# Fourteen instead of eight half tiles of one token quarter's gate and up products inside the last seven segments, with a new table of priorities

## The chip, the cores and the metric

The kernel runs on one core of a Trainium2 chip. The metric is the device time of one execution in microseconds (us). Engines are named as the profile names them: PE (TensorE, matrix products; PEld is its loading of weights), DVE (VectorE), ACT (ScalarE), POOL (GpSimd), SP (SyncE, which mostly issues DMA transfers). SPq and ACTq are the issue of DMA transfers by SP and ACT.

## The reference

Everything is in bf16, with x of 2048 tokens by 640. A layer norm feeds part A, an attention that walks over 64 segments of 32 tokens with 8 memory rows; the memory rows of a segment's output are the memory of the next one, so the segments are strictly one after the other. Part B is a gated network on the layer norm of the sum.

```
for s in range(64):                                  # part A, on layernorm(x)
    h = concatenate([mem, x[32*s : 32*s+32]])        # 40 rows of 640
    q, k, v = h @ Wq, h @ Wk, h @ Wv                 # 32 heads of 128
    p = softmax(masked(q @ k.T * scale))             # the mask is causal among tokens
    o = (p @ v) @ Wo
    mem, out[s] = o[:8], o[8:]
h = x + out
n = layernorm(h)                                     # part B, F = 1728
result = h + (relu(n @ W_gate) * (n @ W_up)) @ W_down
```

## The kernel before, in words

One chain of segments sets the pace. In each segment PE multiplies 32 rows (8 memory rows and the segment's first 24 tokens) with Wq, Wk and Wv (line L1577, 32 columns of the array per matmul and four side by side), takes scores (L1954, L1958), the sums of the exponentials (L1968), the weighted values (L1993, L1998), the product with Wo for the rows that the next segment needs (L2027, L2046) and the sum that turns to the next memory (L2063, L1555). The remaining eight tokens of each segment are handled for several segments together: their q, k and v in `rest`, their output rows in `rest_o` (L1661, written to memory by `rest_out`, L1675). A block z is 128 tokens, four segments; z runs from 0 to 15.

Part B works on quarters of 512 tokens. F is cut into 14 tiles of 128 columns (the last of 64). `ahead` (L1726) computes one half tile, gate or up of one tile, inside a segment, while PE still has the segments' work to do: five chunks of four matmuls of 32 columns each (L1742), 20 in all. It loads that tile's weights by SP (L1731) into Wgs or Wus, one buffer each; the gate half is evacuated with a relu (L1750), the up half multiplied to it (L1756) and the tile stored to scr_g (L1758). The table GXS says for each of the first three quarters from which segment to which, and how many half tiles. Quarters 0 and 1 run 27 each (all of them) in segments 21 to 55; quarter 2 runs eight, declared in segments 56 to 62 (the second number is not included; the scheduler may place the work later). What is not computed early follows behind the last segment.

The end part consists of `gates` (L1761) for what is left of quarter 2 and all of quarter 3, and `downs` (L1809), the product with W_down, for each quarter. In `gates` a tile is two groups of five matmuls that use the whole array (L1778), evacuated by ACT (relu, L1800) and DVE (product, L1802). Its first tile is `done`, half the third entry of GXS (L1765); the tiles computed early are loaded back from scr_g into gT (L1767). Block 15's output rows are inserted ahead of the tile `done + 3` (L1785 to L1788). The order of the calls is gates(2), downs(2), downs(0), downs(1), gates(3), downs(3).

The weights of the end part share memory with Wq, Wk, Wv and Wo, so they can be loaded only as those come free. `load_f` (L2160) issues them on SP: Wg and Wu come in three pieces of columns, FPIECES; the first piece waits for Wq's last use, the others also for the evacuation of the last segment's output:

```
FPIECES = ((512, 896), (896, 1664), (0, 512))
for n, (f0, f1) in enumerate(FPIECES):
    for wt, src, nm in ((Wg, B_W_gate, "Wg"), (Wu, B_W_up, "Wu")):
        load_f(..., ["B0"] + [("osb", 1)] * (n > 0), D * (f1 - f0) * 2)
```

Tiles 4 to 6 are columns 512 to 895, tiles 7 to 12 are 896 to 1663, and tiles 0 to 3 are 0 to 511. W_down (Wd, L2169) follows them, then the narrow last tile (Wl) and the results of quarters 0 and 1 (gTs, L2177).

No order is written out by hand. Every operation is declared with `op(...)`, its name, its inputs and its buffers; a list scheduler (`_Sched`, L817) then goes through modelled time and picks, engine by engine, the ready operation of the highest level: the longest path to the end plus a bias from the table BIAS, by name ("gx") and by name and segment ("gx@57"), in L985 and L986. The table ENGINE says which of ACT and DVE an evacuation runs on. Each engine then runs its list strictly in order, with semaphore waits. Within one SP list a transfer that waits holds back every transfer behind it.

At the start the first tokens are loaded and normalised, and Wq, Wk and Wv arrive chunk by chunk; PE meanwhile runs the early blocks of `rest` beside segment 0. Their q and k are stored to scr_qk by DMAs that ACT issues (L1607), their v to scr_v by SP (L1624).

Of the kernel before, what the change touches and what calls it, by code (L numbers as in the profile page):

```python
# [20 lines left out]
GXS = ((21, 38, 27), (39, 55, 27), (56, 63, 8))  # L21
# [6 lines left out]
BIAS = {"sel2": -428.53, "ezero": 827.13, "ldxs0": 772.6, "ldxs1": -1075.19, "ldxa": 977.15, "ldxl": -444.97,  # L28
    "ldxx": 94.56, "ldxn": 296.11, "ldxx0": -425.81, "ldxst": -946.28, "ldxxm": -329.88, "ldmev": -440.02,
# [18 lines left out]
    "gx": -75.13, "gxrelu": -736.07, "gxev": -228.23, "gxst": -268.67, "ln2nd": -1166.07, "xnld": 1080.06,  # L48
    "gld": -294.56, "gu": 52.5, "relu": 1032.72, "gmul": -789.51, "roz": -16.73, "tn2go": 142.03,
# [1214 lines left out]
def build_kernel(nc, A_x, A_mem0, A_Wq, A_Wk, A_Wv, A_Wo, A_seg_len, B_x, B_W_gate, B_W_up,  # L1264
# [46 lines left out]
    sel2 = ar.alloc("sel2", [128, 64], BF16)  # L1311
# [21 lines left out]
    oTr = [ar.alloc(f"oTr{i}", [128, H, 32], BF16) for i in range(2)]  # L1333
# [547 lines left out]
    for nm, b in (("ldxr", 9000.0), ("ldxr1", 8950.0)):  # L1881
        for t in ("", "s0", "s1", "a", "l", "x", "n", "T", "e"):
            sc.bias[nm + t] = b
# [369 lines left out]
```

## Time and profile before

| | us |
|---|---|
| median of 3 runs | 998.62 |
| lowest, highest | 998.56, 999.2 |
| profiled execution | 995.62 |
| its span | 993.9 |
| PE busy in the span | 973.8 |
| end of segment 0 | 86.95 |
| end of segment 55 | 788.07 |
| end of segment 62 | 861.71 |
| end of segment 63 | 874.21 |

The end of a segment is the start of the first PE group behind its last L1555 matmuls, in the span's time. A row of the timeline gives the start, the length, engine, line, operation, the tiles (out<-in), the number of instructions, and in brackets the idle time ahead of it with what ended it. Lengths of neighbouring PE groups overlap, because matmuls are pipelined; what a group costs is the time from its start to the start of the next one. Rows of DMA issue (SPq, ACTq) give the time that the issuing engine spent; how long a transfer takes to land is in a separate view.

### The profile page before, as it was taken

To read this page: it belongs to the slowest core of one execution; us is meant where nothing else is said; L and a number is where in the kernel's file an instruction comes from. 1 tells how busy PE (TensorE), PEld (TensorE's weight loads), DVE (VectorE), ACT (ScalarE), POOL (GpSimd) and SP (SyncE) were. 2 spreads that over 40 slices of the span, in tenths; PEclk is the share of its full clock that TensorE was granted. 3 is DMA by queue.
4 is the path that set the end of the run, shared out by engine and by line. 5 is a ranking of instruction groups with operands and counts; after the bars stand their busy time and mean duration, and the time that the engine had idled before them with its cause. 6 is when DMAs were issued, how large, how long until landed. Compare 5 with 4: busy or idle time off the path is not lost.

```text
span 993.9 us, 54620 instructions
## 1 busy us (share of the span) xinstructions
PE 973.8 (98%) x25518; PEld 535.7 (54%) x24540; DVE 618.3 (62%) x1345; ACT 502.4 (51%) x1226; POOL 112.5 (11%) x264
## 2 busy tenths in 40 slices
PE   7989999999999999999999999999999999999998
PEld 4334565555555555655555556555555565543343
DVE  5835767768676766576666676767656766523232
ACT  2236555556565565555555565555555656521020
POOL 2341011111011011001000010000100000100000
PEclk9999999999999999999999999999999999999999
DMA  8996122223131323232232234333223352289211
GB/s 320 403 350 145 45 57 57 66 53 92 36 89 39 85 76 83 55 81 66 67 84 62 78 105 86 86 93 79 52 72 89 76 102 76 68 260 288 72 41 40
DMA packets 181553, 103.62 MB, mean 104 GB/s; under 512 B 126212, under 2 KB 177484, under 8 KB 181324
## 3 DMA queue, kind: packets, MB, share of 16 engines
q1 hardware_dynamic: 175948, 95.51, 34.5%
q10 hardware_dynamic: 5376, 4.63, 1.4%
q8 instruction: 196, 3.21, 1.3%
q14 instruction: 33, 0.27, 0.1%
HBM read 67.30 MB, written 29.75 MB: 98 GB/s over the span
## 4 chain that ended last, share of the span: by engine, by line
PE 90%; DMA 4%; SPq 3%; DVE 1%; issue 1%; ACT 0%; POOL 0%; ACTq 0%; DVEq 0%; POOLq 0%
PE ps L1577 49%; PE ps L2046 7%; PE ps L1742 7%; PE ps L2027 7%; PE ps L1834 4%; PE ps L1661 3%; PE ps L1778 3%; PE ps L1993 3%; DMA scr_qk<-stg 3%; PE ps L1555 2%; PE ps L1968 2%; PE ps L1954 1%; SPq L2164 1%; DMA Wq<-in_A_Wq_dram 1%; DMA scr_o<-osr 1%
## 5 line engine op out<-in xcount | busy, mean ns | idle before, releaser
L1411 ACT ACTIVATE tok<-ps 128x512 bf16<-128x512 f32 x216 | 128.2, 597 | 146.5 <-PE ps L1577 141.4
L1577 PE MATMUL ps<-Wk,xT 128*32 128x512 bf16 x2560 | 180.4, 379 | 0.4 <-ACT tok L1411 0.4
L1577 PE MATMUL ps<-Wv,xT 128*32 128x512 bf16 x2560 | 176.3, 379 | 0.0
L1577 PE MATMUL ps<-Wq,xT 128*32 128x512 bf16 x2560 | 170.1, 379 | 0.5 <-DVE tok L1412 0.3
L2076 DVE STREAM_TRANSPOSE QT<-tok 128x512 bf16<-128x512 bf16 x128 | 90.6, 708 | 47.5 <-ACT tok L1411 45.4
L1577 PEld LDWEIGHTS ps<-Wq,xT 128*32 128x32 bf16 x2560 | 70.6, 97 | 66.5 <-DVE xT L1691 9.1
L2076 DVE STREAM_TRANSPOSE KT<-tok 128x512 bf16<-128x512 bf16 x128 | 90.8, 709 | 24.6 <-ACT tok L1411 22.7
L1577 PEld LDWEIGHTS ps<-Wk,xT 128*32 128x32 bf16 x2560 | 68.4, 96 | 55.6 <-DVE xT L1691 2.9
L1963 ACT ACTIVATE E<-ps 128x224 bf16<-128x224 f32 x128 | 45.7, 357 | 81.4 <-PE ps L1958 77.7
L2046 PE MATMUL ps<-Wo,oT 128*32 128x160 bf16 x4096 | 83.5, 233 | 1.0 <-issue 1.0
L2046 PEld LDWEIGHTS ps<-Wo,oT 128*32 128x32 bf16 x4096 | 74.1, 97 | 15.5 <-ACT oT L1411 5.6
L2027 PE MATMUL ps<-Wo,oT 128*32 128x320 bf16 x2048 | 81.5, 300 | 0.9 <-DVE oT L1412 0.8
L1577 PEld LDWEIGHTS ps<-Wv,xT 128*32 128x32 bf16 x2560 | 61.0, 96 | 38.8 <-ACT tok L1411 0.7
L1412 DVE CAST oT<-ps 128x320 bf16<-128x320 f32 x124 | 55.0, 485 | 42.9 <-PE ps L1998 36.9
L1940 POOL COPY QT<-RS 128x256 bf16<-128x256 bf16 x64 | 25.7, 402 | 470.4 <-PE ps L1958 470.2
L1411 ACT ACTIVATE Vm<-ps 128x512 bf16<-128x512 f32 x122 | 72.0, 591 | 11.4 <-PE ps L1577 6.3
L1412 DVE CAST tok<-ps 128x512 bf16<-128x512 f32 x104 | 68.7, 661 | 9.6 <-PE ps L1577 9.3
L2027 PEld LDWEIGHTS ps<-Wo,oT 128*32 128x32 bf16 x2048 | 52.7, 96 | 27.3 <-DVE oT L1412 7.7
L1688 DVE CAST_PREDICATED xm<-turn,ps 128x64 bf16<-128x64 uint16 x126 | 27.9, 222 | 61.3 <-PE ps L1555 61.1
L2011 POOL COPY oTr<-oT 128x128 bf16<-128x128 bf16 x128 | 41.0, 320 | 193.5 <-ACT oT L1411 110.4
L1411 ACT ACTIVATE oT<-ps 128x320 bf16<-128x320 f32 x132 | 50.4, 436 | 11.5 <-PE ps L1998 11.1
L1411 ACT ACTIVATE ps<-seed 128x384 f32<-128x384 bf16 x117 | 54.4, 489 | 2.1 <-DVE half L2035 1.8
(108 smaller groups left out, 1453.5 us busy)
## 6 DMA issues: line engine op xcount, KB each, us to landing
RS<-scr_qk SPq DMA_DIRECT2D x63, 128.0 KB, 2.3
big<-in_A_x_dram SPq DMA_DIRECT2D x34, 160.0 KB, 2.8
Wq<-in_A_Wq_dram SPq DMA_DIRECT2D x10, 512.0 KB, 7.7
Wk<-in_A_Wk_dram SPq DMA_DIRECT2D x10, 512.0 KB, 8.2
Wv<-in_A_Wv_dram SPq DMA_DIRECT2D x10, 512.0 KB, 8.6
Wo<-in_A_Wo_dram SPq DMA_DIRECT2D x8, 640.0 KB, 11.2
Wgs<-in_B_W_gate_dram SPq DMA_DIRECT2D x30, 160.0 KB, 3.0
Wus<-in_B_W_up_dram SPq DMA_DIRECT2D x30, 160.0 KB, 2.9
```

What stands on the lines that cost most here:

```text
L1411: return e.activation(dst, src, ACTF.Copy)
L1412: return e.tensor_copy(dst, src)
L1577: o = pe.matmul(out, lhs[c], rhs, start=(c == 0), stop=(c == DC - 1), skip_group_check=True)
L1661: o = pe.matmul(bank(bk)[p0:p0 + 32, 0:2 * SLICE], oTr[b][:, h, :], cols(h, 2 * a, 2 * a + 2), start=(h < 2), stop=(h >= H - 2), skip_grou ...
L1742: o = pe.matmul(bank(bk)[32 * i:32 * i + 32, 0:512], wt[:, c, 32 * i:32 * i + 32], xn2T[0][:, :, c * 128:(c + 1) * 128], start=(c == 0), s ...
L1778: o = pe.matmul(bank(bk)[:, 0:TB], lhs(c), xT[:, :, c * 128:(c + 1) * 128], start=(c == 0), stop=(c == DC - 1))
L1834: pe.matmul(bank(ba)[:, 0:512], lhs, Wd[:, j, 0:512], start=(j == 0), stop=(j == FC - 1), skip_group_check=True)
L1963: op("act", lambda a: a.activation(E[:, g, :, 0:56], sco(BS[g]), ACTF.Exp, scale=SCALE), r=["table"], w=[("E", g)], x=[BS[g]], dur=0.36, n ...
L2011: op("pool", lambda e: e.tensor_copy(oTr[ob][:, 16 * g:16 * g + 16, XR * y:XR * y + XR], oT[:, 16 * g:16 * g + 16, 0:XR]), r=[("oT", g, 0) ...
L2027: o = pe.matmul(bank(BA)[p0:p0 + 32, 0:2 * SLICE], oT[:, h, XR:40], cols(h, 2 * b2, 2 * b2 + 2), start=(i == 0 and jj < 2), stop=(i == 3 a ...
L2046: o = pe.matmul(bank(BW)[32 * j:32 * j + 32, 0:SLICE], oT[:, 16 + 4 * jj + i, XR:40], cols(h, j, j + 1), start=(i == 0 and jj == 0), stop= ...
L2076: op("dve", lambda v, tb=tb, dst=dst: v.transpose(dst, tok[tb.at][:, :].rearrange("p (h r) -> p h r", r=32)), w=[("QT" if p == 0 else "KT" ...
```

## The change

The third entry of GXS becomes 14, so `done` becomes 7: tiles 0 to 6 of quarter 2 run inside the segments, two half tiles in each of seven, and gates(2) begins at tile 7. gT is loaded with seven tiles instead of four, and block 15's output rows stand ahead of tile 10 instead of tile 7. FPIECES is unchanged. Both tables, BIAS and ENGINE, are replaced in whole, some 750 lines of numbers, and the biases of the first loads (names that begin with ldxr) can now be set by the table.

```diff
-GXS = ((21, 38, 27), (39, 55, 27), (56, 63, 8))
+GXS = ((21, 38, 27), (39, 55, 27), (56, 63, 14))
...
-BIAS = {"sel2": -428.53, "ezero": 827.13, "ldxs0": 772.6, "ldxs1": -1075.19, "ldxa": 977.15, "ldxl": -444.97,
...
     for nm, b in (("ldxr", 9000.0), ("ldxr1", 8950.0)):
         for t in ("", "s0", "s1", "a", "l", "x", "n", "T", "e"):
-            sc.bias[nm + t] = b
+            sc.bias[nm + t] = BIAS.get(nm + t, b)
```

How the new tables move instructions shows only in the order that the scheduler makes of them. The counts of PE's instructions differ in two lines alone: 1360 for 1240 of L1742, 200 for 230 of L1778. Behind the last segment PE's list before is gates(2) from tile 4 (Wg x10, Wu x5, Wg x5, Wu x10, ...), block 15's output rows, the last tiles, 40 of block 14's output-row matmuls, downs(2). After, it is the last 8 gate and 20 up matmuls of tile 6 by `ahead`, then gates(2) from tile 7 (Wg x10, Wu x5, Wg x5, Wu x10), block 15's output rows, Wg x10, Wu x5, Wg x5, Wu x10, downs(2), with the narrow last tile inside downs(2); block 14's output rows all stand in the segments.

SP's list after, around the end of segment 63: first pieces of Wg and Wu, Wgs and Wus of tile 6, the store of tile 5, block 14's output rows, second pieces of Wg and Wu one behind the other (the first of them waits for the evacuation of the last output), two transposed loads (L1771), the store of tile 6, two loads for block 14's layer norm, the last segment's output, third pieces of Wg and Wu, gT, the store of block 14's sum, Wd, Wl. Before, one second piece stands ahead of the two transposed loads and the other behind them, and gT stands behind Wd and Wl.

At the start, ACT's list holds the exponentials of segment 0 (L1963) ahead of the last block of scr_qk stores instead of behind it, that block has five stores behind V's fourth evacuation instead of seven, and the two copies of the first normalised tokens (xr) are on DVE instead of one on ACT. On PE both sums of segment 0 (L1968) stand ahead of the V products of Wv with xr.

More of the change, by code (lines that the diff above doesn't have):

```diff
@@ L27 @@
 FPIECES = ((512, 896), (896, 1664), (0, 512))
-BIAS = {"sel2": -428.53, "ezero": 827.13, "ldxs0": 772.6, "ldxs1": -1075.19, "ldxa": 977.15, "ldxl": -444.97,
-    "ldxx": 94.56, "ldxn": 296.11, "ldxx0": -425.81, "ldxst": -946.28, "ldxxm": -329.88, "ldmev": -440.02,
[18 rows of a table removed]
-    "gx": -75.13, "gxrelu": -736.07, "gxev": -228.23, "gxst": -268.67, "ln2nd": -1166.07, "xnld": 1080.06,
-    "gld": -294.56, "gu": 52.5, "relu": 1032.72, "gmul": -789.51, "roz": -16.73, "tn2go": 142.03,
[632 rows of a table removed]
-ENGINE = {"ldxre": "act", "ldxr1e": "act", "ldmev": "act", "er0ev": "dve", "er0Tev": "act", "er1ev": "act",
-    "ervev": "act", "r0ev": "dve", "r0Tev": "act", "r1ev": "act", "rvev": "dve", "Q0ev": "act", "Q0Tev": "act",
-    "K0ev": "act", "K0Tev": "act", "V0ev": "act", "Q1ev": "dve", "Q1Tev": "dve", "K1ev": "act", "K1Tev": "act",
-    "seed0": "act", "seed1": "act", "oTev0": "dve", "oTev1": "act", "osrev": "act", "ldxre@0": "act",
[81 rows of a table removed]
+BIAS = {"sel2": -468.5, "ezero": 397.8, "ldxrs0": 9556.22, "ldxrs1": 9299.62, "ldxra": 8157.09,
+    "ldxrl": 8663.75, "ldxrx": 9076.13, "ldxrn": 9101.63, "ldxrT": 9580.86, "ldxre": 9514.39, "ldxs0": 2261.81,
+    "ldxs1": -1029.95, "ldxa": 854.49, "ldxl": -268.86, "ldxx": 357.13, "ldxn": 223.78, "ldxx0": -48.42,
[20 rows of a table added]
+    "gx": -76.02, "gxrelu": -589.09, "gxev": 150.7, "gxst": -333.11, "ln2nd": -1210.98, "xnld": 1157.81,
+    "gld": 118.19, "gu": -305.11, "relu": 1424.28, "gmul": -365.48, "roz": -5.91, "tn2go": 413.61,
[634 rows of a table added]
+ENGINE = {"ldxre": "dve", "ldmev": "act", "er0ev": "dve", "er0Tev": "act", "ervev": "act", "r0ev": "dve",
+    "r0Tev": "act", "r1ev": "act", "Q0Tev": "act", "K0Tev": "act", "Q1ev": "dve", "Q1Tev": "dve",
+    "K1Tev": "act", "seed0": "act", "seed1": "act", "oTev0": "dve", "oTev1": "act", "osrev": "act",
[84 rows of a table added]
 class _Slot:
```

1469 rows, old and new, of tables (BIAS, ENGINE) are left out of this document.

## The prediction

> **What bounds the kernel now.** I read the page's busy shares and chain first, then TensorE's timeline through the last segments and the tail, then the DMA queue's own timeline beside it, and last the start.
>
> ```profile
> span 993.9 us, 54620 instructions
> PE 973.8 (98%) x25518; PEld 535.7 (54%) x24540; DVE 618.3 (62%) x1345; ACT 502.4 (51%) x1226; POOL 112.5 (11%) x264
> PE 90%; DMA 4%; SPq 3%; DVE 1%; issue 1%; ACT 0%; POOL 0%; ACTq 0%; DVEq 0%; POOLq 0%
> ```
>
> TensorE is busy for 98% of the span and is 90% of the chain. What is left for a reordering is its idle time, so I asked for its busy time by stretches: start and segment 0; segments 1 to 55; 56 to 62; tail, with segment 63 left out. Columns are window, length, then PE, PEld, DVE, ACT and POOL.
>
> ```profile
> 0.00:86.95 86.95, 75.10 (x1521) 35.86 (x1513) 49.23 (x93) 31.96 (x72) 26.80 (x54) 0.98 0.98 332
> 86.95:788.07 701.12, 697.93 (x20684) 401.85 (x20004) 479.13 (x1067) 403.51 (x1000) 76.57 (x186) 1.00 0.29 72
> 788.07:861.71 73.64, 73.64 (x2197) 44.13 (x2118) 45.66 (x101) 44.40 (x109) 6.30 (x18) 1.00 0.35 79
> ...
> 874.21:993.90 119.69, 115.05 (x786) 47.38 (x572) 36.67 (x68) 16.48 (x31) 0.00 (x0) 1.00 0.47 143
> ```
>
> Segments 56 to 62, into which the change puts work, have no idle TensorE time (73.64 of 73.64 us). Idle time is found in the start (11.85 us), in 1 to 55 (3.19 us in 55 segments) and in the tail (4.64 us). Whatever is moved into the late segments lengthens them by its own cost.
>
> **The half tiles.** Six more half tiles run early: the order of TensorE's instructions holds 120 more of L1742 (32 columns of weights, four side by side) and 30 fewer of L1778 (128 columns); every other matmul count is as before. Their prices are start to start, from these rows:
>
> ```profile
> 849.44 1.03 PE L1742 MATMUL ps<-xn2T,Wgs 128*32 128x512 bf16 x16
> 850.30 0.60 PE L1577 MATMUL ps<-Wk,xT 128*32 128x512 bf16 x8
> ...
> 874.21 2.33 PE L1778 MATMUL ps<-xn2T,Wg 128*128 128x512 bf16 x10
> ...
> 878.54 2.32 PE L1778 MATMUL ps<-xn2T,Wu 128*128 128x512 bf16 x10
> 880.70 2.32 PE L1778 MATMUL ps<-xn2T,Wg 128*128 128x512 bf16 x10
> 884.22 1.25 PE L1778 MATMUL ps<-xn2T,Wu 128*128 128x512 bf16 x5 [1.21 <-DMA Wu<-in_B_W_up_dram]
> ```
>
> 16 of L1742 take 0.86 us, 0.054 each; 10 of L1778 take 2.16 us, 0.216 each. So 120 x 0.054 = 6.5 us are added and 30 x 0.216 = 6.5 us removed: 0 on TensorE. The six evacuations (three relu, three multiply) that change places go where ScalarE is busy 44.40 and VectorE 45.66 of 73.64 us; both cover them, and uncovered each would cost some 0.6 us. The six weight loads of 160 KB and three stores of 128 KB fall where the DMA share is 0.35; I count them 0, and return to them among the rivals.
>
> **What the order does at the end of segment 63.** Call that end T (874.21 before). The last early half tile is not finished at T: 28 of its matmuls stand behind it, 28 x 0.054 = 1.5 us. Then the first product of the third quarter's rest is tile 7, no longer tile 4. The weights come in three pieces of columns; the first, issued early, holds tiles 4 to 6, which this quarter no longer needs. Tile 7 is in the second piece, and that piece is issued only when the last segment's output has been evacuated. The rows of DMA issue and of the evacuation, and then the queue's medians from issue to landing:
>
> ```profile
> 874.32 0.30 ACT L1411 ACTIVATE osb<-ps 128x160 bf16<-128x160 f32 x1 [1.75 <-PE ps L1555]
> ```
> ```profile
> 874.65 0.37 SPq L2164 DMA_DIRECT2D Wg<-in_B_W_gate_dram  x1
> 875.06 2.94 SPq L1771 DMA_TRANSPOSE xn2T<-scr_n  x2
> 878.04 0.58 SPq L2164 DMA_DIRECT2D Wu<-in_B_W_up_dram  x1
> ...
> 879.38 0.59 SPq L2164 DMA_DIRECT2D Wg<-in_B_W_gate_dram  x1
> 880.02 0.76 SPq L2164 DMA_DIRECT2D Wu<-in_B_W_up_dram  x1
> 880.82 6.12 SPq L2164 DMA_DIRECT2D Wd<-in_B_W_down_dram  x2
> ```
> ```profile
> Wd<-in_B_W_down_dram SPq DMA_DIRECT2D x1, 2080.0 KB, 13.3
> Wg<-in_B_W_gate_dram SPq DMA_DIRECT2D x1, 960.0 KB, 5.3
> Wu<-in_B_W_up_dram SPq DMA_DIRECT2D x1, 960.0 KB, 6.1
> Wg<-in_B_W_gate_dram SPq DMA_DIRECT2D x1, 640.0 KB, 6.7
> Wu<-in_B_W_up_dram SPq DMA_DIRECT2D x1, 640.0 KB, 7.9
> ```
>
> Landings before, from T: gate piece two 874.65 + 5.3 = T + 5.7; up piece two T + 9.9; gate piece three T + 11.9; up piece three T + 13.7; Wd T + 19.9. Transfers of one queue land one after the other: 640 KB in 1.84 us (348 KB per us), and 3360 KB from T + 9.9 to T + 19.9 (337).
>
> Before, tile 4's products cover the first landing, and TensorE waits only for the up piece: 880.70 to 884.22 is 3.52 us for 2.16 us of matmuls, 1.4 lost. In the changed order:
> - Gate piece two still lands at T + 5.7; TensorE is done at T + 1.5. Wait: 4.2 us. Behind it in order stand the rest of the gate and up products and the second part's output rows, none of which can pass it.
> - Ten gate products, to T + 7.9. The up piece is now issued right behind the gate piece, not behind the transposes: 960 KB / 340 = 2.8 us later, T + 8.6. Wait: 0.7.
> - 50 products at 0.216 and 64 output-row matmuls, which took 2.3 us:
>
> ```profile
> 892.96 2.36 PE L1661 MATMUL ps<-Wo,oTr 128*32 128x320 bf16 x64
> 895.25 1.25 PE L1778 MATMUL ps<-xn2T,Wg 128*128 128x512 bf16 x5
> ...
> 910.17 0.39 PE L1834 MATMUL ps<-Wd,gT 128*128 128x512 bf16 x1 [0.36 <-DVE osr L1670]
> ```
>
>  That ends at T + 21.7, and the down products follow, which need Wd. On the queue Wd now stands behind gT (896 KB, not 512 and not after Wd), the last early tile's store (128 KB) and two rows' loads (320 KB): from T + 8.6, (3360 + 1344) / 337 = 14.0 us, T + 22.6, up to T + 23.5 if the transposes' 320 KB take their turn in it too. Wait: 0.9 to 1.8; I take 1.2.
>
> Sum of these waits: 4.2 + 0.7 + 1.2 = 6.1 us. Gone are the 1.4 above and the 0.36 at 910.17, since the output rows of that block come earlier. The tail therefore loses 6.1 - 1.8 = 4.3 us; the bounds are 4.2 - 1.8 = 2.4 (the other two waits vanish) and 5.0 (Wd at T + 23.5).
>
> **The start.** The new priorities also reorder the start, which the description hardly mentions. In the old one, TensorE and ScalarE:
>
> ```profile
> 58.65 9.88 PE L1577 MATMUL ps<-Wv,xr 128*32 128x512 bf16 x176
> 70.07 0.25 PE L1968 MATMUL ps<-E,bones 128*32 128x160 bf16 x4 [1.55 <-ACT E L1963]
> ...
> 70.75 2.12 PE L1577 MATMUL ps<-Wv,xr 128*32 128x512 bf16 x20 [0.39 <-ACT lnS L1976]
> 73.45 4.95 PE L1577 MATMUL ps<-Wv,xr 128*32 128x512 bf16 x80 [0.58 <-ACT stg L1411]
> 78.24 1.25 PE L1577 MATMUL ps<-Wq,xr 128*32 128x512 bf16 x20
> 80.29 1.05 PE L1577 MATMUL ps<-Wq,xr 128*32 128x512 bf16 x16 [0.80 <-DVE tok L1412]
> ```
> ```profile
> 66.00 3.61 ACTq L1607 DMA_DIRECT2D scr_qk<-stg  x5
> ...
> 72.81 0.60 ACT L1411 ACTIVATE stg<-ps 128x512 bf16<-128x512 f32 x1 [1.74 <-DMA scr_qk<-stg]
> ```
>
> The first exponential (L1963) stands in ScalarE's order behind the block of stores that it issues from 66.00 on (3.61 us for 5, 0.72 each), and the sums that need it stop TensorE: 58.65 + 176 x 0.054 = 68.15, next start 70.07, 1.9 lost; 0.5 more by 70.75. Then V's products wait for their evacuations, which wait for buffers that those stores free: 70.75 to 80.29 is 9.54 us for 120 matmuls, 6.48, so 3.1 lost. In the changed order both exponentials and sums stand ahead of these V products (Wv with xr), and five stores, not seven, stand between V's fourth and fifth evacuation. The 2.4 us of the first two waits leave; but the fifth evacuation is bound by the stores, which come only 2 x 0.72 = 1.4 us sooner, and what TensorE wins ahead of it, it may lose waiting for free banks. Bounds: 0 (the stores set the end anyway) and 5.5 (all of it goes). I take 1.9, between 1.4 and 2.4.
>
> **The middle.** 3.19 us idle in 55 segments is all a new order could win there, and a slip of a few hundredths in each would lose as much. Either way within 1.5 us; I take 0.
>
> **Sum.** The profiled run took 995.62 us (span 993.9 and 1.7 around it), 3.0 under the median of 998.62. 995.6 + 4.3 - 1.9 = 998.0; with the 3.0, 1001.0 us.
>
> **The rivals.**
> - Faster: the whole 5.5 of the start and 1.5 of the middle are won against 4.3 in the tail: -2.7, 995.9. For it: the first wait sits on an order that the change visibly mends. Against: the 3.1 hang on stores which must still be issued.
> - Even: start and tail cancel (2.4 to 4.3 each): 998.6.
> - Slower still, by a late load in segment 63. The early tiles have a single buffer for gate and one for up weights, each refilled only when TensorE has read the last tile; the last pair's loads are issued behind the unneeded first piece (2 x 480 KB, 2.8 us at 340). By the order the gate load has about 5 us to its first use, counted in matmuls. It decides from there: if it is later, TensorE stops ahead of T too, by up to 2.8: 1003.8.
> - Clock. The 4.2 us wait is longer than any this trace has after the start, and the first matmuls of all ran slowly:
>
> ```profile
> 2.62 1.05 PE L1889 MATMUL ps<-E,ident 128*32 128x512 bf16 x8 [2.62 <-POOL ident L1443]
> 3.44 3.62 PE L1893 MATMUL ps<-E,ident 128*32 128x160 bf16 x124
> 6.90 0.39 PE L1897 MATMUL ps<-E,ident 128*32 128x512 bf16 x4
> 7.11 0.45 PE L1541 MATMUL ps<-ident,big 128*32 128x128 bf16 x20
> ```
>
>  8 take 0.82 us (0.103 each), 4 of the same later 0.21 (0.053). Should the array fall to that half rate after the wait, the slow time is at most the 4.3 us from 2.62 to 6.90, so at most 2.1 are lost; but the waits for the up piece and Wd (0.7 + 1.2) take in all but 0.2 of it: 1001.2, or 1003.1 if those two are absent. I call it 1002.5. [...]
>
> **How the numbers follow.** Forecast 1001.0: chance 0.40 (0.31 beyond 0.2%, which is 2 us and about what a measurement of this kernel can tell from no change, and 0.09 within). Faster 0.25 (0.22 beyond, 0.03 within). Even 0.18. Late load 0.09. Clock 0.08. So faster 0.22, within 0.30, slower 0.31 + 0.09 + 0.08 = 0.48. The forecast's own range is 998.6 (tail 2.4, start -2.4) to 1003.6 (tail 5.0, start 0). The range goes down to 995.8, the faster rival's time, and up to 1004.2, just over the late load.
>
> **What would show it.** TensorE idle for about 4 us some 1.5 us behind the last segment's output, released by the DMA of Wg; a short wait at the first up products and one at the first down products, released by Wu and Wd; segments 56 to 63 longer by 6.5 us together without new idle time; the start's sums not stopped by ScalarE, and segment 0 ending near 85 us. The forecast is wrong if gate piece two lands much before T + 5.7, or if segment 0 ends before 83 or after 87 us.

## The result, and the profile after

| | us |
|---|---|
| kernel before, median (lowest, highest) | 998.91 (998.56, 999.42) |
| changed kernel, median (lowest, highest) | 1013.03 (1012.69, 1018.07) |
| ratio, 95% interval | 1.0154 (1.0135 to 1.0172) |
| changed kernel once more, on another occasion | 1011.8, ratio 1.0117 (1.0082 to 1.0152) |
| profiled execution, before and after | 995.62, 1018.07 |

The changed kernel is slower by 12 to 14 us. The profiled execution of before lies 3 us under its median and that of after 5 us over its own. Stretches compared between these two profiles therefore show some 8 us more in all than the medians do. Below, stretches are read from the profiles, and sizes are settled by experiments on medians.

First TensorE's busy time by stretches: the four of before that match those of after (start and segment 0; segments 1 to 55; 56 to 63; tail). The first and the last row of before stand in the prediction; its two middle ones, cut at the true end of segment 55, are here. (The 788.07 called the end of segment 55 ahead of the prediction is that of segment 56: the stretch called "56 to 62" there held six segments. Segment 55 ends at 776.14.)

```profile
86.95:776.14 689.19, 686.02 (x20328) 395.29 (x19657) 469.44 (x1043) 395.62 (x980) 75.46 (x183) 1.00 0.29 72
776.14:874.21 98.07, 97.68 (x2908) 57.16 (x2805) 62.94 (x141) 58.35 (x143) 10.19 (x27) 1.00 0.34 82
```

After, the same four stretches:

```profile
0.00:91.19 91.19, 77.86 (x1525) 37.38 (x1517) 57.27 (x105) 25.18 (x60) 26.90 (x55) 0.96 0.93 317
91.19:785.20 694.01, 689.94 (x20363) 403.05 (x19693) 469.93 (x1052) 396.93 (x982) 75.11 (x183) 1.00 0.29 73
785.20:890.36 105.16, 102.83 (x3009) 61.37 (x2904) 64.28 (x142) 57.35 (x138) 10.31 (x27) 1.00 0.36 81
890.36:1016.30 125.94, 112.35 (x742) 45.31 (x530) 35.67 (x67) 13.82 (x26) 0.00 (x0) 0.96 0.45 140
```

Lengths grew by 4.24, 4.82, 7.09 and 6.25 us, 22.4 together, which is all of 1018.07 - 995.62. Work moved between them: out of the tail went 30 matmuls of L1778 (30 x 0.216 = 6.5) and block 14's 40 output-row matmuls (40 x 2.3/64 = 1.4), and 28 early ones came in (1.5). So 6.4 us of work left the tail, which nevertheless became 6.25 longer: 12.6 us are lost there. The segments took in 6.4 and grew by 11.9: 5.5 lost. The rest is the start.

Where the tail loses it, in TensorE's timeline (T, the end of segment 63, is now 890.36; lines are 7 higher, so L1778 is L1785 here):

```profile
890.79 1.25 PE L1749 MATMUL ps<-xn2T,Wus 128*32 128x512 bf16 x20
896.07 4.45 PE L1785 MATMUL ps<-xn2T,Wg 128*128 128x512 bf16 x10 [4.03 <-DMA Wg<-in_B_W_gate_dram]
900.31 2.09 PE L1785 MATMUL ps<-xn2T,Wu 128*128 128x512 bf16 x5
902.24 1.24 PE L1785 MATMUL ps<-xn2T,Wg 128*128 128x512 bf16 x5
...
938.34 0.39 PE L1841 MATMUL ps<-Wd,gTs 128*128 128x512 bf16 x1 [4.15 <-DVE tl L1848]
```

and its busy time and granted clock (the third column from the right) around the two long waits:

```profile
895.00:900.00 5.00, 3.93 (x10) 1.46 (x11) 0.00 (x0) 0.60 (x1) 0.00 (x0) 0.52 1.12 347
900.00:905.00 5.00, 5.00 (x20) 2.02 (x19) 2.58 (x6) 1.69 (x4) 0.00 (x0) 0.80 1.10 355
...
938.30:940.00 1.70, 1.66 (x11) 0.64 (x6) 0.38 (x2) 0.00 (x0) 0.00 (x0) 0.87 0.81 292
940.00:943.00 3.00, 2.78 (x12) 0.84 (x6) 0.00 (x0) 0.00 (x0) 0.00 (x0) 0.50 0.79 211
```

- 4.03 us for the gate weights, landing at 896.02 = T + 5.7, as forecast.
- The array then runs at a granted clock of 0.52: ten products take 900.31 - 896.07 = 4.24 us for 2.16, five more 1.93 for 1.08. 2.9 lost. No wait for Wu is left: issued at 891.32, it landed 7.4 us later, at 898.7, ahead of the end of the slow products at 900.31.
- 1.53 us at 916.05 for Wd, which landed at T + 25.7.
- 4.15 us at 938.34, 48 us behind T, for DVE's sum into tl, the tile of output rows. Behind it the clock is at 0.87 for 1.70 us and at 0.50 for 3.00: 1.7 lost.

Sum 4.0 + 2.9 + 1.5 + 4.15 + 1.7 = 14.3. The old waits that went (1.8) and the 12.6 make 14.4, so this is the tail's whole loss in this profile. The wait at T + 48 was in no part of the forecast. SP's list and DVE's timeline ahead of it:

```profile
917.41 2.01 SPq L2184 DMA_DIRECT2D gTs<-scr_g  x2
919.46 8.22 SPq L1723 DMA_DIRECT2D scr_n<-big  x1
927.73 0.43 SPq L1709 DMA_DIRECT2D big<-in_A_x_dram  x1
928.20 0.45 SPq L1711 DMA_DIRECT2D big<-scr_o  x1
```
```profile
934.99 0.49 DVE L1713 TENSOR_TENSOR big<-big,big 128x640 bf16<-128x640 bf16 x1 [7.36 <-DMA big<-scr_o]
936.56 0.64 DVE L1848 TENSOR_TENSOR tl<-tl,ps 128x512 bf16<-128x512 bf16 x1
937.60 1.08 DVE L1848 TENSOR_TENSOR tl<-tl,ps 128x512 bf16<-128x512 bf16 x3
```

The gTs loads are 2 x 1664 KB. The small store behind them keeps SP for 8.22 us, so block 15's two loads are issued only at 927.73, and land 6.76 us after their issue, against a median of 2.6 for this load. In DVE's list block 15's sum (L1713) stands ahead of the sums (L1848) that evacuate the down products' banks (the parts of ps that products are written to): it waits 7.36 us, and TensorE, which needs these banks, waits 4.15 us for DVE's tl. On the queue the 3.3 MB of gTs stand ahead of block 15's loads: they took 13.6 us from issue to landing in the median, to about 931, and the small load behind them landed at 928.20 + 6.76 = 934.96. The chain of waits runs through the rows of L1723 and L1709 above and through these:

```profile
909.74 5.76 DMA scr_o<-osr
...
928.20 6.76 DMA big<-scr_o
934.99 0.50 DVE big L1713
```

At the start, what TensorE waited for in the first 91 us (us in total, times, longest), before and then after:

```profile
PE ps L1577 <- ACT xr L1411: 1.8, 1, 1.8
PE ps L1968 <- ACT E L1963: 1.8, 2, 1.5
PE ps L1577 <- DVE tok L1412: 1.8, 4, 0.8
PE ps L1577 <- DMA Wq<-in_A_Wq_dram: 1.7, 3, 0.9
...
PE ps L1577 <- ACT stg L1411: 0.6, 1, 0.6
PE ps L1577 <- ACT lnS L1976: 0.4, 1, 0.4
```
```profile
PE ps L1584 <- DVE tok L1419: 4.3, 8, 0.9
PE ps L1584 <- DMA Wq<-in_A_Wq_dram: 3.4, 3, 1.6
...
PE ps L1584 <- ACT stg L1418: 0.5, 1, 0.5
```

The sums no longer wait for ScalarE (1.8 and 0.4 gone), as forecast, and its copy of xr (1.8) is no longer waited for. But DVE now carries 105 instructions of the start instead of 93 and ACT 60 instead of 72. Waits for DVE's copies into tok grew from 1.8 to 4.3, and those for Wq's DMA from 1.7 to 3.4: what was won is given back. The clock differs as well: in the first 17 us the granted clock is 0.83, against 1.00 before. And the start scatters: segment 0 ends between 86.17 and 89.98 in the seven profiles with the old start, and between 87.94 and 91.19 in the ten with the new one.

### The profile page after: what moved, and what is told of

It is laid out like the page before. It is cut to its first block, busy times and chain, and to the rows that moved or that the text cites. A ratio compares the mean times of both kernels' runs of the same rounds, so it can differ in the third digit from the quotient of the medians.

```text
span 1016.3 us, 54804 instructions
## 1 busy us (share of the span) xinstructions
PE 983.0 (97%) x25598; PEld 547.1 (54%) x24630; DVE 627.2 (62%) x1366; ACT 493.3 (49%) x1205; POOL 112.3 (11%) x264
## 4 chain that ended last, share of the span: by engine, by line
PE 85%; DMA 4%; SPq 2%; DVE 1%; ACT 1%; issue 1%; ACTq 0%; POOL 0%; DVEq 0%; POOLq 0%
PE ps L1584 45%; PE ps L1749 7%; PE ps L2053 7%; PE ps L2034 7%; PE ps L1785 4%; PE ps L1668 3%; PE ps L1841 3%; PE ps L2000 3%; PE ps L1562 2%; PE ps L1975 2%; PE ps L1961 1%; DMA scr_qk<-stg 1%; DMA xn2T<-scr_n 1%; SPq L1723 1%; DMA big<-scr_o 1%
## 5 line engine op out<-in xcount | busy, mean ns | idle before, releaser
L1418 ACT ACTIVATE tok<-ps 128x512 bf16<-128x512 f32 x204 | 121.5, 596 | 146.7 <-PE ps L1584 134.8
L1584 PE MATMUL ps<-Wk,xT 128*32 128x512 bf16 x2560 | 182.5, 379 | 0.2 <-ACT tok L1418 0.2
L1584 PEld LDWEIGHTS ps<-Wq,xT 128*32 128x32 bf16 x2560 | 74.3, 97 | 63.3 <-DVE xT L1698 9.8
L1584 PEld LDWEIGHTS ps<-Wk,xT 128*32 128x32 bf16 x2560 | 71.8, 96 | 51.7 <-DVE xT L1698 2.0
L1419 DVE CAST oT<-ps 128x320 bf16<-128x320 f32 x132 | 58.6, 485 | 42.7 <-PE ps L2005 37.9
L1419 DVE CAST tok<-ps 128x512 bf16<-128x512 f32 x116 | 77.1, 665 | 12.4 <-PE ps L1584 12.1
L1947 POOL COPY QT<-RS 128x256 bf16<-128x256 bf16 x64 | 25.8, 403 | 473.7 <-PE ps L1965 463.5
L1749 PE MATMUL ps<-xn2T,Wgs 128*32 128x512 bf16 x700 | 55.4, 381 | 0.8 <-DMA xn2T<-scr_n 0.8
```

Source lines behind the costliest of these rows:

```text
L1418: return e.activation(dst, src, ACTF.Copy)
L1419: return e.tensor_copy(dst, src)
L1584: o = pe.matmul(out, lhs[c], rhs, start=(c == 0), stop=(c == DC - 1), skip_group_check=True)
L1749: o = pe.matmul(bank(bk)[32 * i:32 * i + 32, 0:512], wt[:, c, 32 * i:32 * i + 32], xn2T[0][:, :, c * 128:(c + 1) * 128], start=(c == 0), s ...
```

## The experiments

In the two kernels that change GXS alone, the scheduler makes the order anew. In all others every engine's list is kept as it was, and only the moves shown are made. Times are medians; a ratio is to runs of the kernel before on the same chip at the same occasion.

| run | median, us | ratio (95%) |
|---|---|---|
| e7_before_again | 999.64 | 0.9998 (0.9986 to 1.001) |
| e1_again | 1011.8 | 1.0117 (1.0082 to 1.0152) |
| e2_pieces | 1012.39 | 1.0123 (1.0092 to 1.0155) |
| e3_block15 | 1012.65 | 1.0106 (1.0062 to 1.015) |
| e4_tail3 | 1014.54 | 1.0143 (1.0112 to 1.0175) |
| e5_early | 1011.58 | 1.012 (1.01 to 1.014) |
| e10_tailfix | 1006.03 | 1.0067 (1.0048 to 1.0086) |
| e6_oldhead | 1021.48 | 1.0209 (1.0179 to 1.0239) |
| e8_newstart | 1000.8 | 1.0009 (0.9996 to 1.0022) |
| e9_new8 | 1008.66 | 1.0098 (1.008 to 1.0116) |
| e12_old14 | 1029.12 | 1.0304 (1.0286 to 1.0322) |
| e11_before_best | 1004.58 | 1.0052 (1.0033 to 1.0071) |
| e13_head44_new | 1002.05 | 1.0022 (1.0007 to 1.0036) |
| e14_head44_old | 1008.69 | 1.0093 (1.0065 to 1.0122) |
| e15_before_wu | 999.09 | 0.9986 (0.9971 to 1.0001) |

**The two kernels again, their lists replayed unchanged.**

> The kernel before, to see how much idle time the start and the segments have in another execution. In its first profile: 15.8 us in the start, 13.2 in segments 1 to 55, 2.2 in 56 to 63, 2.7 in the tail. Theory: within 1 us of these in each. Rival: start and segments 2 to 3 us more, the rest of its median's 3.0 us over that profile.

> The changed kernel itself, once more, since its profiled execution (1018.07 us) was 5 us above its other three (1012.7 to 1013.3). Theory: those 5 us are in the start, where 40 of Wq's products took 4.24 us for 2.16 at full clock; a usual execution loses none of it, so segment 0 ends near 88 us instead of 91.2, the tail is as in the profile (122.7 us from the end of segment 63 to the last matmul, against 116.6 before) and the time is 1013 (+14). Rival: the 5 us are spread over the segments; then segment 0 ends at 91 again.

Both reproduce. The four stretches of e7_before_again take 87.67, 690.16, 98.13 and 119.44 us. By busy time TensorE is idle in them for 11.67, 3.60, 0.34 and 4.39 us, against 11.85, 3.17, 0.39 and 4.64 in the first profile; the idle times in the expectation are not counted this way.

The second profile of the changed kernel has the same three waits (4.10 for Wg, 2.57 for Wd, 1.98 for DVE's tl). Its tail takes 124.08 us, so 10.8 are lost there instead of 12.6. Its segment 0 ends at 88.88, not 91.19, so some of the 4.24 us at the start is scatter. The half clock behind the wait for Wg costs less here: the next products start at 898.66, 3.85 us behind these, so 1.7 are lost instead of 2.9 (granted clock 0.66 from 894 to 899).

```profile
894.81 4.02 PE L1785 MATMUL ps<-xn2T,Wg 128*128 128x512 bf16 x10 [4.10 <-DMA Wg<-in_B_W_gate_dram]
```

**Take the first wait away.**

```diff
-FPIECES = ((512, 896), (896, 1664), (0, 512))
+FPIECES = ((896, 1280), (1280, 1664), (0, 896))
```

> Only the columns of the three weight pieces are changed (896..1279, 1280..1663, 0..895), so that the piece issued early holds tiles 7 to 9; every engine's order stays. Theory A (the waits add up): the wait for the gate piece (4.2 us), the half clock behind it (2.1) and the wait for the up piece go, so about 7 us less than the changed kernel: 1006. Theory B (one queue): the bytes ahead of Wd in the queue stay the same, so TensorE only waits longer for Wd, and nothing is gained but a little: 1012 to 1013, with a wait of some 9 us at the first down product.

The first piece now holds tiles 7 to 9. The 4 us wait is gone, and the time is not. Waits of TensorE from there to the end:

```profile
PE ps L1793 <- DMA Wd<-in_B_W_down_dram: 6.3, 1, 6.3
PE ps L1737 <- DVE gT L1761: 1.7, 2, 0.9
```

TensorE reaches the down products sooner, Wd lands no sooner, and 6.3 us pass there in place of 4.03 + 1.53. Behind this wait the granted clock is 0.50 from 915.60 to 920.00, which loses another 2.2 us. The wait for Wg had cost little of its own: it was cover for Wd.

**Take the wait at T + 48 away.**

```diff
 SP, behind the second loads of Wl
+tl<-scr_h x4, big<-in_A_x_dram, big<-scr_o
 gTs<-scr_g x2 (1664 KB each)
-tl<-scr_h x4 ahead of these, big<-in_A_x_dram and big<-scr_o behind scr_n
 scr_n<-big
```

> Only SP's order is changed at one place: the four loads of block sums that stand behind block 15's go, and block 15's two loads for its layer norm, now stand ahead of the two large loads of quarters 0 and 1 (3.3 MB). Theory: VectorE's add for block 15 then no longer holds the evacuations of the down products back, so the 4.15 us wait at 934 us and the slow products behind it (about 2 us) go: 6 us less, 1007. Rival: quarters 0's and 1's results then land later and downs(0) waits for them instead: 1011 or more.

TensorE's waits in the tail:

```profile
PE ps L1737 <- DMA Wg<-in_B_W_gate_dram: 4.1, 1, 4.1
PE ps L1793 <- DMA Wd<-in_B_W_down_dram: 3.0, 1, 3.0
```

Block 15's wait is gone; its tail, 118.7 us to the last matmul, is 2 shorter than in the changed kernel run again (120.6). In the median nothing is seen of it: the interval is 9 us wide, so this gain is neither shown nor excluded.

**Wd sooner.**

```diff
 SP (with the pieces of e2_pieces)
 Wg, Wu second pieces
+Wd
 xn2T<-scr_n x2
 ...
-Wg, Wu third pieces
 gT
+Wg, Wu third pieces
-Wd
```

> The pieces of e2, and Wd issued right behind the second piece, with the third pieces behind gT; block 15 as in the changed kernel. Theory A: the first two waits go, with the half clock: 9 us less, 1004. Theory B: block 15's stores and loads still land when the same bytes have gone through the queue, so the wait at VectorE's add grows by most of what was won: 1010 to 1013.

Wd is in time and the sum of block 14 is not: its loads now stand behind Wd, DVE waits 13.5 us for them, and the products' evacuations stand behind it in DVE's list.

```profile
902.81 0.49 DVE L1665 TENSOR_TENSOR big<-big,big 128x640 bf16<-128x640 bf16 x1 [13.52 <-DMA big<-in_A_x_dram]
```
```profile
904.63 1.86 PE L1737 MATMUL ps<-xn2T,Wg 128*128 128x512 bf16 x4 [7.21 <-DVE gT L1761]
...
934.07 0.39 PE L1793 MATMUL ps<-Wd,gTs 128*128 128x512 bf16 x1 [3.13 <-DVE tl L1800]
```

**The pieces before T, then the whole chain.** In the first kernel the second pieces do not wait for the last output's evacuation and are issued 3.5 us ahead of T, Wd stands behind block 14's loads, the third pieces behind gT, and block 15's loads as in e3_block15. The second one has three more moves.

```diff
-load_f(..., ["B0"] + [("osb", 1)] * (n > 0), D * (f1 - f0) * 2)
+load_f(..., ["B0"], D * (f1 - f0) * 2)
 e10_tailfix besides, on SP:
+Wu second piece behind block 14's output rows
+scr_n<-big and xn2T<-scr_n of block 14 ahead of the first gTs<-scr_g
+the second gTs<-scr_g behind xn2T<-scr_n of block 15
```

> The changed kernel with one idea in SP's list: the second pieces of Wg and Wu no longer wait for the last segment's output (the memory is free since Wq's last use) and are issued behind the last early tile's weights, some 4 us ahead of the end of segment 63; Wd follows the two loads for block 14's norm, gT follows Wd, the third pieces follow gT; block 15's loads as in e3. Theory (the tail's 13 us are waits for transfers that come too late, in series): second pieces land by T + 3, Wd by T + 13, block 15's add is not late; TensorE's waits in the tail shrink from 11 to 13 us to 3 or less, so 1002 to 1004, against 1011.8 for the changed kernel. Rival: the waits move to the next transfer again (block 14's add, gT, the quarters' results): 1009 or more.

> e5, and in SP's list three further moves: the up part of the second piece behind block 14's output rows; block 14's norm store and its transposed load ahead of the two large loads of quarters 0 and 1; the second of these behind block 15's transposed load. Theory (waits in series behind one queue): with the late chain of blocks 14 and 15 out of the way the idle time in the tail falls from 11.9 us (e5) to 4 or 5, so 1004 to 1005. Rival: yet another wait takes its place: 1009 or more.

e5_early gains nothing in the median: its waits are now 1.57 (Wu), 2.2 (DVE's gT), 0.74 (Wl) and, 51 us behind T, a new one for block 14's transposed norm:

```profile
938.30 1.99 PE L1737 MATMUL ps<-xn2T,Wl 128*128 128x512 bf16 x5 [3.63 <-DMA xn2T<-scr_n]
```

e10_tailfix serves that chain too and is the only change of the tail whose median shows a gain. Its ratio is 1.0067 against 1.0117 for the changed kernel run again, 5 us less, though the two intervals still touch (1.0086 and 1.0082). Its profile lies 3.4 us over its median; the tail loses 119.71 - 119.69 + 6.4 = 6.4 us there, against 10.8 in e1_again. Its largest waits are 2.0, 1.8 and 1.6. Behind the first of them, for a transposed norm, products are still slow: a down product takes 0.38 us ahead of it and 0.63 behind it.

```profile
933.63 0.38 PE L1793 MATMUL ps<-Wd,gTs 128*128 128x512 bf16 x1
...
936.04 1.25 PE L1737 MATMUL ps<-xn2T,Wl 128*128 128x512 bf16 x5 [1.98 <-DMA xn2T<-scr_n]
...
939.57 0.63 PE L1793 MATMUL ps<-Wd,gTs 128*128 128x512 bf16 x1
```

**How much is the start and the segments?**

```diff
 e8_newstart:    +changed kernel's lists through segment 0,  then before's
 e6_oldhead:     +before's lists through segment 55, then the changed kernel's
 e13_head44_new: +changed kernel's lists through segment 44, then before's
 e14_head44_old: +before's lists through segment 44, then the changed kernel's
```

> The mirror of e6 for the start: the changed order through segment 0, then the order of the kernel before. Forecast on record: the new start saves 1.9 us, so 997. Theory after the first profiles: it costs 1.7 to 4, from TensorE's waits in K's products and the later first pieces of Wq: 1001 to 1003.

> Every engine follows the order of the kernel before through segment 55, and then the changed order. Theory: of the 18.8 us by which e1's profiled execution ends later than before's, 1.7 are new idle time in the start and 4.5 in segments 1 to 55, so 6 us come back: 1006. Rival: those 6 us are what one execution differs from another (the profiled one of before is 3 us under its median): 1010 to 1012.

> The changed kernel's order from the start through segment 44, then the kernel before's order to the end; at that point both have done the same operations, so the join moves nothing else. Theory one (the new order also costs time ahead of the tail, in the start and in segments 1 to 44): 2.5 to 4 us slower than before, 1002 to 1003.5, with the tail at its old 116.5 us. Rival (what is lost is lost behind segment 44, and the idle time seen ahead of it is scatter of profiled executions): within 1.3 us of before, as with the new start alone.

> The mirror: the kernel before's order through segment 44, then the changed kernel's. Theory one: 1008 to 1009.5, that is 2.5 to 4 us under the changed kernel's 1012 to 1013, with its tail of 120 to 123 us and the waits for Wg, Wd and block 15's sum unchanged. Rival: 1011.5 to 1013.

e6_oldhead failed as an experiment: at the join it has a stop of its own (9.85 us at 789.50 for Wgs), so it says nothing of the head. The new start costs 0.9 us (-0.4 to 2.2): no change is within the interval, the forecast gain of 1.9 is not. At the end of segment 44 the two orders have done exactly the same operations. The new order up to there costs 2.2 us (0.7 to 3.6), between what the theory and its rival wanted, with an interval that reaches into both; everything behind it costs 9.3 us (6.5 to 12.2), with e14_head44_old's median of 1008.69 where the first theory had it. Together 11.5, about the whole of e1_again. The tail of e14_head44_old has the three waits:

```profile
PE ps L1737 <- DMA Wg<-in_B_W_gate_dram: 4.2, 1, 4.2
PE ps L1514 <- DMA Wd<-in_B_W_down_dram: 2.7, 1, 2.7
PE ps L1793 <- DVE tl L1800: 1.9, 1, 1.9
```

and its segments 56 to 63 and tail by stretches:

```profile
779.37:885.33 105.96, 103.33 (x3011) 62.18 (x2905) 64.30 (x142) 57.23 (x138) 10.30 (x27) 1.00 0.36 80
885.33:1006.90 121.57, 109.60 (x742) 44.63 (x530) 35.62 (x67) 13.82 (x26) 0.00 (x0) 0.99 0.47 145
```

The tail loses 121.57 - 119.69 + 6.4 = 8.3 us, and idle time in segments 56 to 63 is 2.63, against 0.39 before.

**Half tiles and tables apart.**

```diff
 e9_new8, the changed kernel with the old number of half tiles:
-GXS = ((21, 38, 27), (39, 55, 27), (56, 63, 14))
+GXS = ((21, 38, 27), (39, 55, 27), (56, 63, 8))
 e12_old14, the kernel before with the new number:
-GXS = ((21, 38, 27), (39, 55, 27), (56, 63, 8))
+GXS = ((21, 38, 27), (39, 55, 27), (56, 63, 14))
```

> The new tables alone, with eight half tiles as before (third entry of GXS 8). Through segment 55 the order is that of the changed kernel; behind the last segment TensorE starts at tile 4, whose weights are loaded early. Theory: the tail's waits come from starting at tile 7, so they are gone (2 to 4 us of idle time in the tail, as before) and only the new idle time in the start and the segments is left, 4.7 us in e1 against e7: 1003 to 1005. Rival: the new tables' order of the tail is what costs, with 8 as well: 1009 or more.

> Fourteen half tiles with the tables of before; the scheduler now defers two half tiles (40 matmuls) and all of downs(2) to behind downs(0). Theory: the order that starts at tile 7 must wait for the second piece with any table: some 3 us for the gate piece, then for the first of downs(0), whose quarter-0 results come behind all weights; 1004 to 1010. Rival: the half tiles cost nothing by themselves and the tables do it all: 999 to 1001.

The new tables alone cost 9.8 us with eight half tiles (their longest tail wait is 2.55 us, for Wl), and six more half tiles add 2 to 6 (to 1.0117 and 1.0154, taken on other occasions; the interval of the first overlaps with that of e9_new8). With the old tables they cost 30: waits of 5.3 us for Wg, 8.4 for gTs and 7.6 for gT. So fourteen half tiles need another order than the old one; but the new one is slower than the kernel before with either number.

With eight half tiles the loss lies elsewhere. In the profile of e9_new8 the tail takes 120.42 us with block 14's 1.4 us of work moved out of it, so only 2.1 are lost there, and no wait for Wg is left, as the theory said. But segments 1 to 55 take 695.33 us instead of 689.19, and segments 56 to 63 take 102.02 instead of 98.07, with 4.01 us idle instead of 0.39. So the long waits in the tail come with the start at tile 7, and the new tables have a price of their own ahead of T, larger than the theory's 4.7.

**One wait taken out of the kernel before.**

```diff
 SP
 Wg second piece
+Wu second piece
 xn2T<-scr_n x2
-Wu second piece
 e11_before_best besides:
+scr_o<-osr x2 of block 14 ahead of gTs<-scr_g x2
-scr_o<-osr x2 of block 14 behind them
```

> The kernel before with one move on SP: the up weights' second piece right behind the gate weights' second piece, ahead of the two transposed loads, as the changed kernel has it. Theory one (in the tail each wait stands for itself as long as nothing behind it on the queue is late): the 1.2 to 1.4 us wait for Wu at 884.22 goes and the time falls by 1.0 to 1.4, to 998. Rival (waits on this queue are handed on): the wait comes back behind it, at the transposed loads or at Wd, and the time stays within 0.5 us of before or rises.

> The kernel before with two moves in SP's list: the up part of the second piece directly behind the gate part, ahead of the two transposed loads, and block 14's output rows ahead of the two large loads of quarters 0 and 1. Theory: the waits of 1.2 us (for the up piece) and 0.4 us (for VectorE's osr) in its tail go: 1.5 us or 0.15% less than before. Rival: the tail then waits for a later transfer: no change, or 1 us more.

In e15_before_wu the 1.21 us wait for Wu is gone, and 0.93 us come back at the narrow last tile, T + 22.9:

```profile
880.56 1.24 PE L1730 MATMUL ps<-xn2T,Wu 128*128 128x512 bf16 x5
...
901.31 1.24 PE L1730 MATMUL ps<-xn2T,Wl 128*128 128x512 bf16 x5 [0.93 <-DMA Wl<-in_B_W_up_dram]
```

T to the last matmul takes 116.6 us in both. The ratio's interval, 0.9971 to 1.0001, holds a gain of the wait's size and, just, no change, so the median does not decide; in the profile the tail gains nothing. e11_before_best is slower: gTs is issued later, and a block's load behind it is late for DVE's sum (first DVE, then TensorE), as in the changed kernel:

```profile
924.42 0.49 DVE L1658 TENSOR_TENSOR big<-big,big 128x640 bf16<-128x640 bf16 x1 [4.14 <-DMA big<-in_A_x_dram]
...
928.78 0.39 PE L1786 MATMUL ps<-Wd,gTs 128*128 128x512 bf16 x1 [3.84 <-DVE tl L1793]
```

No version beat the kernel before by more than a measurement can tell.

## Why the prediction was wrong

The forecast was 1001.0 with a range to 1004.2; the median is 1013.03. Its terms were tail +4.3, start -1.9, middle 0.

- **The half tiles on TensorE, "0".** Right in work, wrong in cover. The segments took in 6.4 us of work and lost 5.5 more in the profile (3.9 in e14_head44_old: 2.4 in segments 1 to 55 and 7.9 in 56 to 63, less 6.4). "Segments 56 to 63 longer by 6.5 us without new idle time" failed: 7.09 longer, with idle time up from 0.39 to 2.33, in pieces of 0.8 and less behind a transposed load and evacuations.
- **The wait for Wg, 4.2.** Right: 4.03, 4.10 and 4.16 in three profiles, where forecast and for that reason.
- **"Wait: 0.7" for Wu and the rival of the clock.** The clock rival was given 0.08, and the slow products that it supposed were there behind the wait for Wg in all four profiles in which it lasted 4.0 to 4.2 us: over the 4 or 5 us there the granted clock was 0.52 in the first profile, 0.66 in e1_again and e14_head44_old and 0.69 in e3_block15. They cost 2.9 us in the first profile, where five up products were slow too, 1.7 in e1_again and e14_head44_old and 1.5 in e3_block15, against "at most 2.1". This took in the wait for Wu, as that rival said it would. The prediction's own rows of the start had slow products in them: behind waits of 1.55 and 0.39 us, 20 products from 70.75 on took 2.12 us, where 20 at 78.24 took 1.25 (granted clock 0.56 from 70.75 to 73.00, 0.69 from 73.45 to 75.00 and 1.00 from 78 to 80). By an estimate from these rows and clocks, some 1.5 of the 3.1 us there that were put down to evacuations and stores were slow clock.
- **Wd, "T + 22.6", wait 1.2.** It landed at T + 25.6 to T + 25.8 in four profiles. The wait was small (1.53) only where the slow clock covered the difference; with the clock back sooner 2.57, 2.75 and 3.02. Where the further 3 us of that queue went was not settled.
- **The sum of the tail.** This is the step that failed. It followed TensorE's list and the queue up to Wd, T + 21.7, and stopped. Behind Wd the same SP list goes on to gTs, block 15's loads, DVE's sum, and the banks of the down products; a stop of 4.15 us and 1.7 of slow clock came from there. The queue was followed for Wd and not for what stood behind it. Measured loss 12.6 in that profile, 10.8 in e1_again and 8.3 in e14_head44_old, against 4.3. In e14_head44_old, whose profile lies at its median, the terms that were missing or too small are 1.91 for DVE's tl (put at nothing), 1.7 for the half clock (left to a rival) and 1.55 more for Wd, with 0.7 for Wu to be taken off: 4.3 + 4.5 = 8.8, near the measured 8.3.
- **Waits added and subtracted one by one.** Wrong as a method here. e2_pieces took 4.03 away and got 6.3 for Wd instead of 1.53; e4_tail3 served Wd and got 7.2 for DVE's gT; e5_early got 3.63 for the norm of block 14; e15_before_wu took 1.21 away and got 0.93 at Wl. The loads of the tail go through one SP list and one queue (q1, at 347 and 355 GB/s from 895 to 900 and from 900 to 905 in the changed kernel), and in these four runs the time won at one load was waited for at a later one. Only e10_tailfix, which ordered the whole chain, gave time back in the median.
- **The start, -1.9.** The waits named did go, and the bound of 0 was the right end: e8_newstart costs 0.9 us (-0.4 to 2.2). What was missed is who does the evacuations: 12 instructions went from ACT to DVE, and TensorE waits for DVE instead. No run moves these alone, so this reading of two profiles is not tested. "Segment 0 ending near 85" failed with 91.19 and 88.88.
- **The middle, 0 within 1.5.** The new order through segment 44, start included, costs 2.2 us (0.7 to 3.6): at or over that edge.
- **The late load in segment 63.** It did not happen: no wait for Wgs or Wus ahead of T.

The changed kernel's loss is therefore mostly behind segment 44, 9.3 us of 11.5, and there mostly in the tail; the rest is small idle times in nearly every stretch. With eight half tiles the same tables lose most of their time ahead of T instead. Why the new tables gave an order with these idle times is not shown by any run.

## What to carry to other kernels

Where loads stand in one queue and one in-order list, cost a change by the time at which the queue reaches each user down to the last one, not by adding the waits that are seen now: in e2_pieces the wait of 4.03 us that was removed had been the cover of the next, which grew from 1.53 to 6.3. Look in every in-order list for a long-latency consumer (here a sum that needs a load) that stands ahead of cheap evacuations (0.64 us for one here), because its lateness became TensorE's: 7.36 us of waiting on DVE, 4.15 on TensorE. A wait of TensorE of some 4 us cost its length here and then 1.5 to 2.9 us more, at granted clocks of 0.52 to 0.69.

## What the runs showed of the hardware

The granted clock fell after shorter waits than the 4.2 us of the prediction's clock rival, and not after every one. In e9_new8 a wait of 2.55 us was followed by a clock of 0.51, and in e14_head44_old one of 2.75 by 1.00:

```profile
911.38 2.31 PE L1785 MATMUL ps<-xn2T,Wl 128*128 128x512 bf16 x5 [2.55 <-DMA Wl<-in_B_W_up_dram]
...
911.00:914.00 3.00, 2.62 (x7) 0.82 (x7) 0.00 (x0) 0.27 (x1) 0.00 (x0) 0.51 1.09 346
```
```profile
911.12 0.22 PE L1514 MATMUL ps<-Wd,gT 128*128 128x128 bf16 x1 [2.75 <-DMA Wd<-in_B_W_down_dram]
...
911.00:914.00 3.00, 2.88 (x22) 1.07 (x11) 0.00 (x0) 0.00 (x0) 0.00 (x0) 1.00 0.72 206
```

A wait of 1.98 us was followed by slow products in e10_tailfix (0.63 us for 0.38, its rows are above), and one of 1.91 in e14_head44_old by a granted clock of 1.00 from 929 to 940. In the start of the kernel before, waits of 1.55 and 0.39 us close together were followed by 0.56 from 70.75 to 73.00, and over the whole stretch by 0.84:

```profile
70.00:81.00 11.00, 9.14 (x144) 3.56 (x144) 3.88 (x8) 6.93 (x17) 0.00 (x0) 0.84 1.04 235
```

So in these rows the length of one wait does not decide: a fall came behind 1.98 and 2.55 us as well as behind 4.03, and none behind 2.75. What decides is not shown by any run.

A small store held SP: the 160 KB of scr_n took 8.22 us to issue behind 3.3 MB of gTs, and everything behind it in SP's list stood as long. The next store of this kind, at 937.71, took 0.41.
